# Seven rotating float32 pieces instead of three for the first unit's FFN activations, with the written-out order of all work replaced

## The chip, the cores and the metric

The kernel runs on one core of a Trainium2 chip. The metric is the device time of one execution in microseconds (us). The core has a matrix engine (TensorE, PE in the profile; PEld is its weight load), three elementwise engines (VectorE = DVE, ScalarE = ACT, GpSimd = POOL) and a queue engine (SyncE = SP) that issues transfers. Each works through its own instructions in order and waits on the others by semaphores. Matrix results go to PSUM banks, everything else lives in SBUF.

## The reference, cut to what matters

Attention whose mask comes from hash bits (batch 4, 8 heads, 768 tokens, head size 64), then a feed-forward network (FFN, 512 to 2048 to 512) on the 3072 tokens:

```python
q_bits = (np.einsum('bhsd,dk->bhsk', q, proj) > 0)
k_bits = (np.einsum('bhsd,dk->bhsk', k, proj) > 0)
mask = q_bucket[:, :, :, None] == k_bucket[:, :, None, :]
scores = np.where(mask, scale * q @ k.T, -1000000000.0)
attn = exp(scores - max) / (sum + 1e-09)
x = (attn @ v)                      # to [3072, 512]
h = x @ w_in
g = h * np.tanh(log1p(exp(h)))      # "mish"
return g @ w_out
```

## The kernel before

**Units.** The tokens are worked in 12 units of 256 (four batches of three). A unit has eight attention steps S, numbered 0 to 95 over the kernel, and eight FFN steps m, also 0 to 95. Most operands are split into a float16 high part and a float16 rest, and a product is three matmuls: high by high, high by low, low by high. In the first unit (FFN steps 0 to 7) the FFN instead runs in float32, with one matmul (L1120, L1169) where the later units have three (L1130 to L1132, L1179 to L1181).

**An attention step** S n: the scores of two heads for 128 queries on PE into the banks ps_s (L937, or L948 in float32), the row maximum on DVE (L978, "max"), a few tiny scale instructions ("mb", L961 to L973), two exponentials on ACT (L991), row sums and their reciprocal (L1015, L1021), then from unit 1 on the high part ("hi", L390 on POOL, L392 on ACT or L393 on DVE) and the rest ("lo", L408 on DVE or L414 and L415 on POOL), which transfers turn (DMA_TRANSPOSE), and for every fourth step the product with the values (V, L1088). From S 8 on there is one set of ps_s banks, so S n+1 can start only when both exponentials of S n have read them.

**An FFN step** m: H (24 matmuls, PE) into one of two accumulators acc0, acc1 in turn; mish on ACT out of it (L1151, in the first unit L1147) into a piece of the buffer ffb; from unit 1 on g_hi and g_lo, the float16 halves, into one of four other pieces; and two output products O m 0 and O m 1 (six matmuls each) into ps_o. After every eighth step the output is copied out ("ob", L1197 on ACT or L1203 on DVE) and stored.

**The buffer ffb** has nine pieces of 512 float32. Step m puts its mish into piece m % 3 (line `t = m % 3`). Pieces 3 to 6 hold the float16 halves of the steps of unit 1 and later (3 + m % 4), which the first unit does not have. Piece 7 begins with a unit matrix.

**Tables.** exp and mish lie in different tables of ScalarE. A change is an ACT_TABLE_LOAD (L1315), which `Plan.ordered` puts in wherever the next exp or mish in the order is not of the table that is loaded.

**The order.** Nothing is scheduled at build time. Every operation is registered with its predecessors, worked out from the regions that it reads and writes, and gets a number. ORDER is a written-out list of all 2636 numbers. A letter after a number picks an engine among the operation's alternatives (none is the first, b the second and so on). Each engine's program is its part of this list. The numbers used below: S 15, 16, 17 are 493, 533, 553, and the maximum of S 16 is 534; S 20 and 21 are 659 and 691; S 24, 25, 26, 27 are 794, 826, 842, 871; mish of m 0 to 7 are 398, 400, 457, 459, 524, 526, 587, 589; the four part copies of the last output are 2634, 2632, 2629, 2627. Two tiny matmul groups use a shared bank: a statistic "st" (621) and the hash bits "hp" (568, 627).

```python
if o.kind and o.kind != table:
    table = o.kind
    load(table)
```

Of the kernel before, what the change touches and what calls it, by code (L numbers as in the profile page):

```python
# [93 lines left out]
137 7 9 8 50 20 0 5 11 19 12 22 1 2 3 4 76 80 29 81b 13 37 6 77b 14 15 10 25 33 26 30b 38 17 27 28 18 34 39 52  # L94
60 61 35 62 41 56 54 63 57 55 21 42 48 51 53 24 23 31 78 36 32 64 65 16 86 91 138 92 79 87 147 40 88 82 117 83
43 118 44 119b 93 89 66 109 110 111 153 90 94 120 67 112 154b 132 107d 46 108 133 113 95 115 68 114 116 124
125b 155 121 126 101 84 45 134 136 135 156 127b 178 96 128 140b 148 141 47 58 149 85 122d 123 97 99 142 139b
98b 143 129 168d 179 180d 100 174 176 69 175 177 170 130 157 171b 131 172 173b 204 205b 169 70 145b 182 189
144b 102 158 159 181 161b 190b 71 193 291 194 195 185 191 150 186 192 220 221 103 222d 183b 187 206 160b 196
188 197 104 223 212 152 146 49 151 162 59 105 106 213b 207 216 218 217b 219b 214 215b 184 353 224 243 163 239  # L100
164 244 245b 241 248 240 242 233c 270 368 307 210d 208 235 254 236 255 249 209b 237 246 238 247 225 256 271
250 257 234 272d 262 263 268 266 292 198 273 226 267b 211 227 293 165 294 269 251 283 284 349 350 264 303 265
285 295 166 304b 354 305 296 258 199 200 309d 286b 310 311c 260c 261 306 274 281 313 253 252 232 228 282 312b
322 201 317 364 287 365 288 289 290 366 318 319 355b 323 324 308 320 321 367 330b 331 315 338 339 72 231 203
202 167 229 397 369b 314 329 316 325 297 298b 275 276b 340 333 341 230 332b 334 342 73 370d 299 336 425c 277
74 426 371 399 378 379 380 335 328 302 400 398 300 373 424 423 351 337 301 280 381 427 372b 374 382 389c 411
376 259 375 278 279 406 429 458 428 390 412 452 407 352 391 383 384b 393 392c 395 326 327 385 453 408d 409 410
415d 343 344c 356c 416 451 430 456 345 431 432 394 377 459 386 418 346 457 396 401 417b 454 433 387 348 347
413 419 455 75 357 434 443d 488b 460 421 444 461 420 388 422 441 404 435 436 414 402 445 489 490b 447 437 462d
# [5 lines left out]
589 597 613 599 580 363 618 600 560 561 562 614d 616 584b 615 632c 563 564c 601 566 651 508 509 585 633 647  # L115
634c 648 655 659 640 617 567 649 636 650 652 664 653 605 635 656 565 619 620 621 660 654 638 622 623c 625 568
569 602 639 661d 609 668 606 641 663 662 681b 682 683c 642 626 637 570b 691 607b 608 685 657 665 666 571b 627
692 628 693d 572 624b 643b 782 672 644 645c 646 695 694 669 610b 658 723c 724 629 630b 684b 687 696 734 735
670b 673 783 697 675 725b 727 736d 738 686 726 631 698 737 688 690 689 732 786 731 749 674 667 699c 701 729
740d 741 791 742c 744 676 728 787 788 700 750 751 702 730 745 799 703 704 706 743b 677b 671 678 746 739 733  # L120
# [1225 lines left out]
```

## Time and profile before

| what | us |
|---|---|
| median of 3 runs (lowest, highest) | 817.67 (816.54, 818.07) |
| the profiled execution, own time | 817.2 |
| its span in the profile | 815.4 |
| PE busy in the span | 798.2 |
| ACT busy | 624.9 |
| DVE busy | 602.9 |
| POOL busy | 426.9 |

The profiled execution's time is 1.8 us above its span; all sums over the trace are made against the span. A matmul's busy time contains its way through the array, so neighbouring matmuls overlap: a busy PE says that no gap was seen, and not that it ran at its peak. Idle time is put down to the engine and line whose semaphore came last.

### The profile page before, as it was taken

The numbers are of one execution on the slowest core, as the hardware profiler recorded it, in microseconds if no ns is written. First come the engines' busy times: TensorE is split into PE (matmuls) and PEld (weight loads), VectorE is DVE, ScalarE is ACT, GpSimd is POOL, SyncE is SP. The second block draws the span as 40 slices with busy tenths as digits, with TensorE's granted clock in tenths as the row PEclk, the third lists the DMA queues.
The fourth block names the chain that finished last, engine by engine and source line by source line (L and its number), as shares of the span: only waits on it lengthen the run. The fifth ranks groups of instructions, "written<-read, shape, count | busy, mean of one in ns | idle before, by whom it ended". The sixth has DMA issues, their size and how long they took to land.

```text
span 815.4 us, 17000 instructions
## 1 busy us (share of the span) xinstructions
PE 798.2 (98%) x6546; PEld 549.6 (67%) x6546; DVE 602.9 (74%) x1103; ACT 624.9 (77%) x976; POOL 426.9 (52%) x434
## 2 busy tenths in 40 slices
PE   8899999999999999999999999999999999999998
PEld 5556666666676776676666676667676676776674
DVE  5888999988898778887887767768877675566211
ACT  4889998888696769889679698989779785677211
POOL 3564446554356773733585564344646758845120
PEclk9999999999999999999999999999999999999999
DMA  7958998989999969989989959999989577466200
GB/s 253 219 174 221 240 246 196 191 156 206 217 160 182 203 116 181 170 158 216 185 172 155 195 117 151 197 213 192 167 140 169 107 139 145 81 124 133 50 27 27
DMA packets 395489, 134.29 MB, mean 165 GB/s; under 512 B 365456, under 2 KB 386448, under 8 KB 395408
## 3 DMA queue, kind: packets, MB, share of 16 engines
q1 hardware_dynamic: 395408, 133.21, 81.2%
q8 instruction: 51, 0.84, 0.4%
q14 instruction: 30, 0.25, 0.1%
HBM read 35.65 MB, written 6.29 MB: 51 GB/s over the span
## 4 chain that ended last, share of the span: by engine, by line
PE 47%; ACT 1%; DVE 1%; DMA 1%; issue 0%; POOL 0%; SPq 0%; ACTq 0%; DVEq 0%
PE ps_s L937 7%; PE ps_o L1179 6%; PE ps_o L1181 6%; PE ps_o L1180 6%; PE ps_acc L1130 5%; PE ps_t L1088 5%; PE ps_acc L1132 5%; PE ps_acc L1131 5%; ACT pb L991 1%; DVE svb L978 1%; DMA out_dram<-ffb 1%; PE ps_t L739 0%; ACT L1315 0%; DVE hl L408 0%; ACT tok L480 0%
## 5 line engine op out<-in xcount | busy, mean ns | idle before, releaser
L991 ACT ACTIVATE pb<-ps_s,svb 128x768 f32<-128x768 f32 x184 | 180.9, 987 | 87.4 <-DVE svb L968 36.7
L978 DVE TENSOR_REDUCE svb<-ps_s 128x2 f32<-128x1536 f32 x92 | 161.3, 1753 | 40.2 <-PE ps_s L937 33.7
L1130 PE MATMUL ps_acc<-X,wo 128*128 128x256 f16 x616 | 167.9, 273 | 0.3 <-ACT ffb L1151 0.3
L1132 PE MATMUL ps_acc<-X,wo 128*128 128x256 f16 x616 | 167.9, 273 | 0.0
L1131 PE MATMUL ps_acc<-X,wo 128*128 128x256 f16 x616 | 167.9, 273 | 0.0
L1315 ACT ACT_TABLE_LOAD x117 | 150.1, 1283 | 2.0
L408 DVE SCALAR_TENSOR_TENSOR hl<-pb,svb,hl 128x768 f16<-128x768 f32 x131 | 140.3, 1078 | 13.8 <-POOL hl L390 9.8
L1181 PE MATMUL ps_o<-wi,ffb 128*128 128x512 f16 x352 | 133.4, 379 | 0.0
L1180 PE MATMUL ps_o<-wi,ffb 128*128 128x512 f16 x352 | 133.4, 379 | 0.0
L1179 PE MATMUL ps_o<-wi,ffb 128*128 128x512 f16 x352 | 133.4, 379 | 0.0
L937 PE MATMUL ps_s<-KT,QT 128*128 128x512 f16 (+1 forms) x656 | 120.1, 326 | 2.1 <-ACT pb L991 1.8
L390 POOL TENSOR_SCALAR hl<-pb,svb 128x768 f16<-128x768 f32 x68 | 71.0, 1046 | 75.9 <-DVE svb L1021 28.8
L937 PEld LDWEIGHTS <-QT 128*128 128x128 f16 x672 | 64.2, 98 | 40.5 <-issue 8.3
L1088 PE MATMUL ps_t<-PT,VT 128*64 128x256 f16 x1584 | 90.7, 273 | 0.0
L1088 PEld LDWEIGHTS <-VT 128*64 128x64 f16 x1584 | 84.8, 110 | 8.1 <-issue 7.6
L1151 ACT ACTIVATE ffb<-ps_acc,smalls 128x512 f32<-128x512 f32 x88 | 58.5, 684 | 33.5 <-PE ps_acc L1132 32.0
L415 POOL TENSOR_TENSOR hl<-pb,hl 128x768 f16<-128x768 f32 x45 | 75.0, 1667 | 3.8
L414 POOL TENSOR_SCALAR pb<-pb,svb 128x768 f32<-128x768 f32 x45 | 44.4, 987 | 48.0 <-ACT hl L392 21.4
L1131 PEld LDWEIGHTS <-wo 128*128 128x128 f16 x616 | 60.2, 98 | 13.3 <-issue 1.5
L1130 PEld LDWEIGHTS <-wo 128*128 128x128 f16 x616 | 60.2, 98 | 12.6 <-issue 0.5
L1132 PEld LDWEIGHTS <-wo 128*128 128x128 f16 x616 | 60.2, 98 | 7.0
L1181 PEld LDWEIGHTS <-ffb 128*128 128x128 f16 x352 | 34.4, 98 | 41.6
(240 smaller groups left out, 1300.5 us busy)
## 6 DMA issues: line engine op xcount, KB each, us to landing
out_dram<-ffb SPq DMA_DIRECT2D x22, 256.0 KB, 2.7
stg<-in_v_dram SPq DMA_DIRECT2D x13, 384.0 KB, 4.0
stg<-in_k_dram SPq DMA_DIRECT2D x12, 384.0 KB, 4.0
wo<-in_q_dram SPq DMA_DIRECT2D x9, 512.0 KB, 4.9
stg<-in_moe_w_in_dram SPq DMA_DIRECT2D x8, 512.0 KB, 4.6
stg<-in_moe_w_out_dram SPq DMA_DIRECT2D x6, 512.0 KB, 4.6
PT<-hl SPq DMA_TRANSPOSE x176, 4.1
wo<-in_moe_w_out_dram SPq DMA_DIRECT2D x5, 512.0 KB, 4.7
```

The lines of the kernel that those rows point to most:

```text
L408: return [("DVE", 215 + 1.035 * n, port(lambda: nc.vector.scalar_tensor_tensor(out=dst, in0=src, scalar=sc, in1=hi, op0=ALU.mult, op1=ALU. ...
L937: nc.tensor.matmul(ps[:, hh * S + c0 * P:hh * S + c1 * P], QTb[:, u % 2, sl, qi], KTb[:, j, sl, hh * NCH + c0:hh * NCH + c1].rearrange("p ...
L978: op("max", [("DVE", 1755, lambda: nc.vector.tensor_reduce(out=sv[:, 0], in_=ps.rearrange("p (h e) -> p h e", e=S), axis=AX.X, op=ALU.max, ...
L991: EXP[n, hh] = op("exp", [("ACT", 1075, lambda hh=hh, t=t: nc.scalar.activation(pb[:, t], HOMES[n][0][:, hh * S:(hh + 1) * S], AF.Exp, bia ...
L1088: nc.tensor.matmul(pv[hh * D:(hh + 1) * D, y * 256:(y + 1) * 256], vt[:, w, hh * NCH + c], pt[:, hh, a * NCH + c].rearrange("p s t -> p (s ...
L1130: nc.tensor.matmul(o, wh, X[:, 0, c], start=(c == 0), stop=False)
L1131: nc.tensor.matmul(o, wh, X[:, 1, c], start=False, stop=False)
L1132: nc.tensor.matmul(o, wl, X[:, 0, c], start=False, stop=(c == NCC - 1))
L1179: nc.tensor.matmul(PS[f"o{s}"], gh, wh, start=first, stop=False)
L1180: nc.tensor.matmul(PS[f"o{s}"], gh, wl, start=False, stop=False)
L1181: nc.tensor.matmul(PS[f"o{s}"], gl, wh, start=False, stop=last)
L1315: for fn in plan.ordered("exp", lambda x: nc.scalar.preload_act_table_set(sets[x])):
```

## The change

In the first unit, step m now uses piece m % 7 instead of m % 3, so pieces 3 to 6, which only later units used, take part. Later units keep m % 3. The ORDER list is another one throughout: the same 2636 numbers, in other places and in part with other engine letters. No operation is added or removed apart from the table loads that follow from the order. The code, and the parts of the list around the steps named above ("..." marks what is left out):

```diff
-463 464 478d 403 446c 449 479 405 465 438 466b 471 472b 487 523 518 493 494 495c 486 358 359 467 496 480b 482b
-497 448 481b 484 360 491 510 525 532 511 442 450 361 512b 533 534 535 362 526 524 468 483 513b 492 439 546 514
-474 536 552 485 469 470 537 519b 475c 476 516 473 520 538c 539 553 515 517 586 540b 521 554 440 477 498 499b
...
-500 501 555d 542 522 541c 556 557 573b 574 575 548 549b 550 527 503 502 544 577 590 545 543 578 528 530 504
-505b 591 592 547 588 506 594 593 507 576b 595d 587 581 612 603 604 551 582 583b 579 596 598c 529 559 558 531
...
-634c 648 655 659 640 617 567 649 636 650 652 664 653 605 635 656 565 619 620 621 660 654 638 622 623c 625 568
-569 602 639 661d 609 668 606 641 663 662 681b 682 683c 642 626 637 570b 691 607b 608 685 657 665 666 571b 627
...
-803 781 752 753 773b 800 784c 774 776 775 785 790 679b 804 705b 707 708 710 709 711 794 748 824 712 801c 779
-777b 795 796c 802b 789 713 792 714c 716 780 747 778 825 839 680 798 797 816c 817 818b 715b 819 826 827 828 829
-820 822 830 807 808 842 611 717 754 755 821 847 823 810 831b 832 833b 809 811 756 757 805 843 844 845 835 846
-840 718 859 841 836 834c 719 721b 720b 758 759 860 722 760 837 838 769 861 871 872 863 873b 874 812 862b 864
...
-2608 2603 2607b 2602 2621 2609 2613 2614c 2610b 2611 2616 2617 2618b 2619b 2615 2623 2620 2625 2622 2576 2631
-2579 2634b 2635 2632b 2633 2624 2626 2629b 2627 2630 2628
...
+447 464 487 523 493 446 402 489 437 438 465 466b 403 449b 478 494 479 480c 482 405 495d 496 497 448 481b 450
+442 518 525 439 533 467 526 524 468 483 356c 472c 440 510d 473 511 484 534 535 512b 490 470 469 514 474 536
+475 537 515 485 486 492 359 546 553 513 491 538d 360 539 476 516 519b 520 521 477 498 499b 554 541 540b 500
...
+517 501 542 522 548c 544 555d 557 556 573c 574 362b 575c 577 549 550 552 586 527 587 528 590 547 503 502 504
+505b 529 591 592 543 506 576c 551 578 545 588 581 530 594 593 507 531 508 582b 579 612 559 558 604 603 589 560
...
+561 361 509 583 648 595d 596 597b 598b 613 599 647 614d 615 616 562 363 580 600 618 651 659 609 640 655 563
+564c 566 601 649 652 567 617 632d 633 634 636b 584c 650 585 635 565 605b 660 638 619 620 606 641 656 607b 661d
+621 622 623 653c 654 625 664 568 668 663 662 681c 637 639 602 626 569 608 643c 644 682 645c 691 692 690 627
...
+704 790 705b 706 745 752 707 678 785 709 753 746 710 773c 774 775c 794 777 789 795 800 776b 711 779b 747 778
+780 847 801 781 825 712 748 840 796 798 797 802 713 714c 791 716 816c 804 715c 680 817 819b 805 826 827 828
+818c 820 806 829 830 831c 807 824 717 754 822 808 832 833c 835b 642 755 810 756 757 821 834b 823 836 809 842
+843 811 839 859 718 769 844 837 812c 719 841 884 758 845 846 759 760b 871 887 770 868 891 860d 721b 720b 861
...
+2609 2605 2606b 2610c 2607 2612 2611b 2613 2621 2616 2614 2615 2623 2620 2625 2622 2576 2579 2617 2618 2619
+2631 2634b 2635 2632b 2633 2624 2626 2629b 2627b 2630 2628
...
@@ ffn_mish
-        t = m % 3
+        t = m % (3 if u else 7)
         tr = ("ff", t * 512, (t + 1) * 512)
@@ ffn_out
-        w = (3 + m % 4) * 512 if u else (m % 3) * 512
-        g32, w32 = ffb[:, m % 3], at(HOME[1, g])
+        w = (3 + m % 4) * 512 if u else (m % 7) * 512
+        g32, w32 = ffb[:, m % 7], at(HOME[1, g])
```

Counted over the two lists:

| | before | after |
|---|---|---|
| table changes in all | 117 | 113 |
| of these ahead of S 32 | 24 | 26 |
| groups of mish in the first unit | 1,0 / 3,2 / 5,4 / 6,7 | 0,1 / 3,2 / 5,4 / 6 / 7 |
| g_hi on ACT, POOL, DVE | 34, 34, 20 | 30, 30, 28 |
| hi on ACT, POOL, DVE | 53, 68, 55 | 54, 60, 62 |
| scale instructions "mb" on DVE, POOL | 74, 22 | 64, 32 |

More of the change, by code (lines that the diff above doesn't have):

```diff
@@ L99 @@
[L99 to L103, printed above, removed]
@@ new lines @@
+910 906b 869 912 940 968 941 930b 932 969 942 943 854 903 931c 934 855 976 851b 945d 946 856 1027 907b 857b
+921 972 954 933 948b 955 970c 947 956d 949 958 1028 957 886 935 858 937 936 982 944 951 950 959c 977 938 973
+986 967 960 961b 962b 963 978 1066 979 980 981 995c 974c 983 964 952 965 971 1029c 966 1031b 1005 1004 996 987
+1006 1030c 997c 999 1007d 1008 1009 975b 998 1001b 990 991 992 1010b 1011 1012b 993 994 1021 953 1022 1192
+1193 1032 1194 984b 1014 1023b 1024 1025 1000 1002 1015 1019 1033 1069 1003 1050 1013c 1016b 1034 1039b 1040
@@ new lines @@
+985 1051 1041b 1017 870 1223 1195 988b 1070 1018 1038 1196 1082 1073 1042b 1052d 1053 1043 1054 1055c 1044
+1056 989 1057c 1059 1045b 1058c 1046 1060 1077 1061b 1078 1079c 1083 1074 1081 1080 1063 1020 1086 1064 1035b
+1067 1068 1071c 1072 1075c 1197 1036 1084c 1095c 1096 1098b 1097 1099b 1062 1105 1047 1090 1106 1107c 1108
+1109 1101 1110 1085 1111 1121 1122 1087 1091 1048 1076b 1198 1112c 1123 1124 1114 1125 1150 1151 1088b 1127d
+1037 1065 1100 1113c 1158 1116 1102 1154 1136 1104 1103 1128 1092 1200 1155 1137 1115 1117 1129b 1130c 1138
@@ new lines @@
+1131 1139 1132 1140 1141c 1133 1093 1142 1143b 1145 1134 1146 1119 1168 1159 1160 1161 1163 1162 1177c 1144b
+1147 1152c 1153 1126 1118 1164 1178 1094 1169 1179 1187 1188 1189 1190 1181 1191 1207c 1208 1148 1049 1201
+1120 1172 1180b 1183b 1156 1089b 1165 1166 1157b 1209c 1211 1218 1199 1219 1220b 1173 1175 1224 1182 1210b
+1213b 1184 1252 1212 1174 1225 1176 1226c 1222 1221 1236d 1237 1238 1149 1135 1240b 1228 1186 1185 1216 1202
+1247 1282 1215 1278 1248 1249c 1250 1251 1203 1239c 1205 1214 1253 1229 1241 1286 1204b 1242 1267d 1170 1171
@@ new lines @@
+1409 1361 1388 1263 1389 1390c 1264b 1265b 1392b 1410 1411b 1406 1399c 1414 1347 1327 1346 1412 1413 1431c
+1462 1360 1391c 1394 1362 1393 1395 1266 1441 1348 1354 1403c 1298 1328 1329c 1432 1331 1442 1443c 1433b 1435
+1444 1369 1363 1422 1332 1307 1400b 1445 1446c 1434c 1437 1370 1415 1423 1447 1425 1419 1416c 1448b 1330b
+1450b 1424 1426 1371 1372 1396 1457 1333 1334 1458 1440 1439 1459b 1373 1502 1374 1335b 1404 1336b 1460 1461
+1375 1475 1476 1377 1438 1436 1449 1451 1486 1337 1378 1506 1477 1503 1504b 1515 1379 1454 1452 1407 1479 1487
@@ new lines @@
+1563 1584 1536 1535 1473 1550 1552 1551 1572 1562b 1564 1573 1574c 1597 1559 1428 1527 1566 1429b 1575 1430
+1565 1501 1576 1592 1553 1601 1582 1577 1585c 1578b 1643 1644 1593 1594 1567 1596 1595 1610c 1580 1586 1646
+1681 1611 1579 1568 1620 1618 1621 1645 1598 1613 1599b 1622b 1616 1581 1485 1605 1619 1683 1589 1600 1590
+1623 1647 1612b 1614b 1624 1625 1626 1627c 1629b 1615 1636 1628b 1631b 1633 1634 1635 1606 1637 1607 1638c
+1868 1630 1617 1632 1608 1602 1609 1648 1603 1653 1640 1639 1654c 1655 1656 1657c 1665 1666 1667 1668 1658
@@ new lines @@
+1904 1886 1905 1923c 1888 1846 1850 1859 1890 1871 1933 1887 1889 1924 1847b 1925b 1872 2020 1848b 1894 1873
+1898 1926c 1927b 1934 1860 1935b 1906 1895b 1936 1937 1914 1964 1929 1875 1919c 1953d 1954 1896 1955b 1891
+1965 1917 1915 1916 1966 1957 1920 1899b 1907 1967 1968 1970c 1900b 1849 1938 1930 1928 1876 1910 1932 2012
+1979 1931 1958 1939 2077 1971 1972c 1956 1959 1918 2021 1974 1874b 2013 1940 1911 1973 1941 1980 1877 1878
+2014c 1921 1981d 1879b 1961 1962 1942 1982 1983 1976 1922 1943 1880 1908 1909 1944c 2016 2029 2003d 2017 1912c
@@ new lines @@
+1975 1960 1985 1881 2004 1946 2005c 2007 2024 2025 2026c 2028 2027 2046c 1984 1947 1977 2033 1969 1963 2008
+1948 2056 1949 2015 2018 2006b 1945b 1913b 2011 1986 1987 1951 2057 2009b 2010 1950b 2019b 1988 1978 2055 1989
+2047 2048c 2034 2030 2031b 2049 1990c 2058 2050 2060 2059 2061c 1992 2052 1999 2032 2062 2063c 2037 2072 1861
+1952 1991b 2038 2040 2039 2041 1993 2051 2053 2070 1994 2121 2089 2073 2022 2074 2078 2065b 2075 2076 2064b
+2122 2090d 2035 2036b 1995 2067 2079 2080 2091 2092 2066 2101 1892 2068 2102 2103 2093 2104 2094 2105 2106c
@@ new lines @@
+2117 2000 2114 2054 2082 2107 2096 2023 2125 2069 2134 2071 2126 2001 2206 2002 1996b 2127d 2108 2128 2110
+2129 2123 2143d 2095 2097 2083 2118 2109c 2111 2153 2098 2144 2112 2296 2044c 1997 2084 2085 2154 2155c 2145
+2146c 2147 2156 2115b 2042c 2157 2113 2256 1998 2130 2138 2119 2149 2120 2081c 2158b 2159 2160c 2169 2099 2131
+2045b 2141 2132b 2135 2086b 2133b 2162 2170 2171b 2257 2139 2172 2173 2136c 2150 2148 2161c 2043 2087 2175
+2124 2164 2176 2163 2151 2198 2202 2184 2203 2185 2177b 2178 2199 2179 2297 2186 2188 2181 2137 2088 2165 2166
@@ new lines @@
+2484 2548 2519 2520c 2510c 2499 2551 2515 2509b 2511b 2482 2485c 2513 2514 2512 2522 2521 2524c 2549c 2525
+2486 2550b 2533 2516 2555 2523 2517 2546 2488 2552 2527b 2530b 2490 2526 2528 2553c 2534 2535 2537 2536 2538b
+2539 2529 2541b 2544 2540 2554b 2532 2569 2568 2556 2557b 2558b 2542 2531 2465 2489 2491 2559 2570 2560 2571
+2545 2543 2561c 2562 2572 2573 2563 2577 2574 2564 2565 2566 2567 2580 2581 2582 2584 2585 2586c 2583b 2588
+2592 2589 2578b 2575b 2590c 2593 2594b 2587b 2591b 2595b 2597 2596 2599 2608 2601 2598 2603 2600 2604 2602
```

155 lines of the change are left out of this document (57 added, 98 removed).

## The prediction

> **What bounds the kernel now.** I read the page's busy line first, then busy time by stage (the cuts are the starts of S 0, 10, 20, 31, 64 and 95), then PE in order of time.
>
> ```profile
> span 815.4 us, 17000 instructions
> PE 798.2 (98%) x6546; PEld 549.6 (67%) x6546; DVE 602.9 (74%) x1103; ACT 624.9 (77%) x976; POOL 426.9 (52%) x434
> ```
>
> ```profile
> 0.00:14.90 14.90, 11.84 (x111) 9.02 (x112) 6.71 (x24) 6.78 (x13) 4.62 (x11) 1.00 0.76 265
> 14.90:71.60 56.70, 51.28 (x426) 32.86 (x424) 47.34 (x94) 46.91 (x96) 30.45 (x36) 1.00 0.78 206
> 71.60:158.40 86.80, 86.09 (x523) 58.64 (x522) 80.64 (x121) 79.35 (x119) 44.08 (x39) 1.00 0.98 217
> 158.40:249.50 91.10, 88.13 (x799) 62.50 (x797) 81.88 (x151) 75.02 (x116) 42.42 (x47) 1.00 0.99 188
> 249.50:502.00 252.50, 251.26 (x2150) 174.54 (x2148) 197.30 (x361) 206.57 (x317) 148.07 (x144) 1.00 0.89 169
> 502.00:744.80 242.80, 242.80 (x2068) 168.25 (x2067) 171.38 (x324) 191.15 (x289) 143.46 (x143) 1.00 0.81 152
> 744.80:815.40 70.60, 66.80 (x483) 43.80 (x481) 17.68 (x31) 19.16 (x30) 13.76 (x15) 1.00 0.20 44
> ```
>
> The columns are length, then busy time of PE, PEld, DVE, ACT and POOL, then clock and transfers. Length less PE busy is what PE stood idle: 3.06, 5.42, 0.71, 2.97, 1.24, 0 and 3.80 us, 17.2 in all. So PE sets the time from S 10 on, and whatever is taken off another engine can win at most these gaps. A busy PE could still be a slow one; the order of time shows its pace:
>
> ```profile
> 183.62 0.27 PE L1130 MATMUL ps_acc<-X,wo 128*128 128x256 f16 x1
> ...
> 186.24 0.38 PE L1179 MATMUL ps_o<-wi,ffb 128*128 128x512 f16 x1
> ...
> 187.53 1.46 PE L937 MATMUL ps_s<-KT,QT 128*128 128x512 f16 x8
> 188.84 0.27 PE L1130 MATMUL ps_acc<-X,wo 128*128 128x256 f16 x1
> ```
>
> From start to start, H takes 2.62 us, an O 1.29, an S 1.31, one behind the other without a hole. The change keeps all of this PE work. What it can move is where PE waits:
>
> ```profile
> 171.35 0.46 PE L739 MATMUL ps_t<-pj,KT 128*128 128x12 f16 x12 [0.72 <-DVE hl L408]
> ```
>
> ```profile
> 206.11 0.59 PE L937 MATMUL ps_s<-KT,QT 128*128 128x512 f16 x2 [0.57 <-ACT pb L991]
> ```
>
> ```profile
> 212.03 0.38 PE L937 MATMUL ps_s<-KT,QT 128*128 128x512 f16 x1 [0.41 <-ACT pb L991]
> ```
>
> ```profile
> 217.95 0.59 PE L937 MATMUL ps_s<-KT,QT 128*128 128x512 f16 x2 [0.24 <-ACT pb L991]
> ```
>
> ```profile
> 241.22 0.38 PE L937 MATMUL ps_s<-KT,QT 128*128 128x512 f16 x1 [0.45 <-ACT pb L991]
> ```
>
> These five (before the hash of entry 627, S 25, S 26, S 27, S 30) are 2.39 of the 2.97 us idle between S 20 and S 31.
>
> **The change part by part.** *The seven pieces.* They free the first unit's mish of the wait for the O that last read its piece. There is no such wait to remove: the eight float32 mish waited 0.7 us in all, for their own H.
>
> ```profile
> L1147 ACT ACTIVATE ffb<-ps_acc 128x512 f32<-128x512 f32 x8 | 4.4, 595 | 0.7 <-PE ps_acc L1120 0.7
> L1315 ACT ACT_TABLE_LOAD x117 | 150.1, 1283 | 2.0
> L991 ACT ACTIVATE pb<-ps_s,svb 128x768 f32<-128x768 f32 x184 | 180.9, 987 | 87.4 <-DVE svb L968 36.7 <-DVE svb L965 24.2 <-POOL svb L973 11.7
> L978 DVE TENSOR_REDUCE svb<-ps_s 128x2 f32<-128x1536 f32 x92 | 161.3, 1753 | 40.2 <-PE ps_s L937 33.7 <-PE ps_s L948 3.5 <-ACT tok L480 1.8
> L408 DVE SCALAR_TENSOR_TENSOR hl<-pb,svb,hl 128x768 f16<-128x768 f32 x131 | 140.3, 1078 | 13.8 <-POOL hl L390 9.8 <-ACT hl L392 3.0
> L392 ACT ACTIVATE hl<-pb,svb 128x768 f16<-128x768 f32 x53 | 48.7, 929 | 14.3 <-DMA PT<-hl 6.7 <-DVE svb L978 2.6 <-ACT pb L991 2.6
> L393 DVE TENSOR_SCALAR hl<-pb,svb 128x768 f16<-128x768 f32 x55 | 39.9, 726 | 4.0 <-DMA PT<-hl 3.2
> L607 DVE SCALAR_TENSOR_TENSOR wi<-wi 128x1024 int32<-128x1024 int32 x2 | 2.4, 1204 | 0.0
> ```
>
> Nor do they gather more: with two accumulators a third mish needs an H after the first, and the new list has five groups in the first unit where the old had four. So the change doesn't do what its ring is for, and that is part of my forecast, not a rival. Value 0.
>
> *Table changes.* 117 become 113, at 1.283 us each: 5.1 us less on ACT. Ahead of S 32 there are two more (+2.6), behind it six fewer (-7.7). Behind S 31 PE has only 1.24 us of idle time to give, spread over 495 us, so I take 0 for the six; if ACT did bound that stage they would be worth 7.7. The two more fall where ACT has 7.45 and 16.08 us idle (the third and fourth stage): 0, at most +2.6.
>
> The Trainium skill ("ScalarE: Activation LUTs", What ACT_TABLE_LOAD costs) gives a change about 2.66 us: 1283 ns and a drain of 1380 ns. By it the two early ones would cost 5.3 us on ACT and speak against the change; the trace below has the first ACTIVATE 1.30 us after the load's start (195.52 less 194.22), so no such drain is seen here.
>
> *The waits at S 25, S 26, S 27.* ACT between the exponentials of S 23 and S 24:
>
> ```profile
> 194.22 1.28 ACT L1315 ACT_TABLE_LOAD   x1
> 195.52 0.69 ACT L1151 ACTIVATE ffb<-ps_acc,smalls 128x512 f32<-128x512 f32 x1
> 196.10 1.76 ACT L392 ACTIVATE hl<-pb,svb 128x768 f16<-128x768 f32 x2
> 197.77 0.92 ACT L392 ACTIVATE VT<-stg,smalls 128x768 f16<-128x768 f32 x1
> 198.60 0.66 ACT L1151 ACTIVATE ffb<-ps_acc,smalls 128x512 f32<-128x512 f32 x1
> 200.20 0.84 ACT L480 ACTIVATE tok<-stg 128x768 bf16<-128x768 f32 x1 [0.94 <-DMA stg<-in_k_dram]
> ...
> 201.76 0.84 ACT L480 ACTIVATE tok<-stg 128x768 bf16<-128x768 f32 x1 [0.62 <-DMA stg<-in_v_dram]
> ...
> 202.71 1.28 ACT L1315 ACT_TABLE_LOAD   x1
> 204.01 0.99 ACT L991 ACTIVATE pb<-ps_s,svb 128x768 f32<-128x768 f32 x1
> ```
>
> The new list takes out of this chain two "hi" (1.76), one v_hi (0.92) and one mish (0.66): 3.3 us, against a wait of 0.57. The gap before it holds about 1.0 us more of ACT work in the new list, so the wait is gone even if the two loads come as late as now; 1.7 us later (3.3 - 1.0 - 0.57) it would be back. After it, S 25 to S 26 and S 26 to S 27 each took 5.92 us by the rows above (206.11, 212.03, 217.95), which is how long scores, maximum and exponentials need. PE had S and V, then S, three O and two tiny groups, in between. The new list adds one O to each (entries 824 and 884), 1.29 us against waits of 0.41 and 0.24: both gone. The hash of entry 627, now directly behind S 21, gets an O (690) in front: 1.29 against 0.72, gone. Together -1.94, bounds -1.94 and 0.
>
> *What is late next.* S 28 to S 30: the old list has 16.1 us of PE work (9.49 and 6.65, from the paces above) and 16.6 of ACT work there, and 0.45 of wait. The new one has 13.5 and 14.4, an excess of 0.9: +0.45 (0 to 0.9). S 16: its maximum (534) follows its S at once in the old list; in the new one seven DVE jobs come first, two w_join (1.20 each), one lo (1.08) and four short ones. Much of it runs while PE still works on S 16: +0.3 (0 to the 3.5 us of the three). S 92 to S 93: PE work falls from 9.1 to 6.5 us while ACT gets two mish, two high parts and two table loads, 7.9 us with its exponentials; the work before it leaves some slack: +0.2 (0 to 1.4).
>
> *Engine letters.* 24 tensor_scalar jobs move to DVE (hi 7, g_hi 8, w_hi 4, v_hi 3, q_hi and k_hi 1 each), and ten "mb" leave it. DVE is idle in front of a maximum for 40.2/92 = 0.44 us on the mean; a "hi" takes 0.73. So one that lands ahead of a maximum makes it 0.29 late. I take +0.5 (0 to 2.5, worked out under the rivals).
>
> *The first 71.6 us.* 8.48 us of idle time, mostly turns through one bank. Pairs of turns with at most 0.33 us of other PE work between them: eight in the old list, six in the new, but more of these directly behind each other. Value 0, a quarter of the 5.42 either way (1.4).
>
> *The end.*
>
> ```profile
> 809.05 0.88 DVE L1203 TENSOR_SCALAR ffb<-ps_o,smalls 128x256 f32<-128x256 f32 x2 [9.60 <-PE ps_o L1181]
> 811.64 0.48 DVE L1203 TENSOR_SCALAR ffb<-ps_o,smalls 128x256 f32<-128x256 f32 x1 [1.71 <-PE ps_o L1181]
> ```
>
> ```profile
> 812.16 0.47 ACT L1197 ACTIVATE ffb<-ps_o,smalls 128x256 f32<-128x256 f32 x1 [8.08 <-DVE ffb L1203]
> ```
>
> The last copy moves from ACT to DVE: two on DVE took 0.88, the mixed pair 0.99 (812.63 less 811.64): -0.1.
>
> *Sum.* -1.94 - 0.1 + 0.45 + 0.3 + 0.2 + 0.5 = -0.6, on the profiled execution's 817.2: 816.6, which stands 1.1 us under the runs' median of 817.67.
>
> **The rivals.** *Faster:* nothing takes the place of the waits removed, and the first 71.6 us give their 1.4: 817.2 - 2.04 - 1.4 = 813.8; with the early part alone at 0, 815.2. For it: 27 gaps between scores have under 6.7 us of PE work in the new list (S 20 on; 21 in the old), but none is under 5.92, where the old had two. Against: the early DVE work grows.
>
> *Slower:* the jobs moved to DVE put off row maxima. Place: the gaps between scores of under 6.7 us, 27 of 75. Price: 24 x 27/75 x 0.29 = 2.5 us, which with the gains lost is 819.7. It decides from the point where DVE's idle time in front of L978 falls under what a moved job adds, 0.29 a step. For it: DVE is busy 81.88 of 91.10 and 80.64 of 86.80 us in the two stages between S 10 and S 31. Against: behind S 31 it is busy 78% and 71%.
>
> *ScalarE sets the time behind S 31:* six loads fewer give -7.7, 809.5. Against it: PE's missing gaps there. The Trainium skill ("Perfetto Trace Analysis", Identifying the Most-Contended Engine) would leave room for it: it calls matmul busy share a bad measure and takes weight-load busy, which is 67% here. The pace of 1.29 an O without holes speaks for a full PE all the same.
>
> **How the numbers follow.** 0.2% (1.6 us) is about what a measurement of this kernel can tell from no change, so 816.0 to 819.3 is the same. My forecast, 816.6, lies in it: 0.40. Faster: 0.33 for the first rival, 0.03 for ScalarE. Slower: 0.24 for DVE. The range runs from 812.6 (the first rival's 813.8, and the 1.24 us behind S 31 returned as well) to 820.6 (the slower case and the 0.9 that S 28 to S 30 can cost). The forecast's own range is 815.2 (the waits removed, nothing added) to 818.6 (the waits come back elsewhere and the four added terms, 1.45, stay).
>
> **What would show it.** Right: no wait on L991 of over 0.2 us at S 25, S 26 and S 27; 113 table loads; ACT's busy time down by some 5 to 10 us with PE's unchanged at 798; idle PE behind S 31 still under 2.5 us. Wrong: a wait in front of S 17 or S 30 of over a microsecond; waits of PE on DVE behind maxima all over; or a first stage whose S 10 starts over 1.5 us away from 71.6.

## The result, and the profile after

The changed kernel takes 824.62 us (median of 5 runs, 823.31 to 826.62), the kernel before in the same session 817.08 (816.54 to 818.07): a ratio of 1.0094, interval 1.0077 to 1.0110, so 7.7 us slower (7.5 by the medians). The profiled execution took 825.72, with a span of 823.9, 8.5 over the span before.

The page after, its span and TensorE's busy line:

```profile
span 823.9 us, 16988 instructions
PE 800.2 (97%) x6546; PEld 550.0 (67%) x6546; DVE 613.2 (74%) x1082; ACT 614.4 (75%) x967; POOL 390.8 (47%) x424
```

ScalarE lost 10.5 us of work and GpSimd 36; VectorE got 10.3 more. TensorE, which sets the time, is busy 2.0 us longer with the same 6546 matmuls, and idle 23.7 us in place of 17.2. Busy time by stage, cut at the starts of S 0, 10, 20, 31, 64 and 95 as in the prediction (length, then busy time of PE, PEld, DVE, ACT and POOL, then clock and transfers):

```profile
0.00:14.80 14.80, 11.12 (x106) 8.13 (x106) 4.64 (x21) 5.54 (x13) 2.58 (x8) 1.00 0.85 274
14.80:73.70 58.90, 52.18 (x430) 33.38 (x428) 48.75 (x95) 49.14 (x99) 29.43 (x43) 1.00 0.76 203
73.70:158.40 84.70, 83.35 (x498) 56.50 (x497) 79.83 (x120) 79.13 (x117) 34.63 (x38) 1.00 0.94 211
158.40:250.50 92.10, 90.58 (x822) 64.50 (x821) 82.59 (x140) 77.33 (x120) 47.37 (x48) 1.00 1.00 192
250.50:508.00 257.50, 252.53 (x2149) 175.23 (x2148) 196.44 (x355) 196.84 (x306) 137.26 (x145) 0.99 0.90 167
508.00:750.80 242.80, 241.05 (x2058) 167.31 (x2057) 183.10 (x326) 187.62 (x289) 116.66 (x121) 1.00 0.79 149
750.80:823.90 73.10, 69.36 (x495) 44.97 (x493) 17.88 (x31) 18.83 (x27) 22.91 (x23) 1.00 0.25 51
```

Length less PE busy: 3.68, 6.72, 1.35, 1.52, 4.97, 1.75 and 3.74 us idle, where before had 3.06, 5.42, 0.71, 2.97, 1.24, 0 and 3.80. One stage got better, S 20 to S 31, by 1.45 us. Two stages that had almost no idle time now have it: S 31 to S 64 gained 3.7 us of it, and S 64 to S 95 1.75. PE in order of time, the larger of its waits from S 4 on and the one at S 25 (in brackets how long, and for what):

```profile
37.77 1.24 PE L937 MATMUL ps_s<-KT,QT 128*128 128x512 f16 x7 [0.83 <-DMA KT<-wo]
...
121.34 0.81 PE L948 MATMUL ps_s<-KT,QT 64*128 64x256 f32 x6 [0.76 <-ACT pb L991]
...
206.62 1.46 PE L937 MATMUL ps_s<-KT,QT 128*128 128x512 f16 x8 [0.25 <-ACT pb L991]
...
272.54 1.46 PE L937 MATMUL ps_s<-KT,QT 128*128 128x512 f16 x8 [0.87 <-ACT pb L991]
...
469.71 2.72 PE L937 MATMUL ps_s<-KT,QT 128*128 128x512 f16 x8 [2.54 <-ACT pb L991]
...
500.10 1.46 PE L937 MATMUL ps_s<-KT,QT 128*128 128x512 f16 x8 [0.75 <-ACT pb L991]
...
552.95 1.46 PE L937 MATMUL ps_s<-KT,QT 128*128 128x512 f16 x8 [0.74 <-ACT pb L991]
...
567.20 0.16 PE L496 MATMUL ps_t<-smalls,ones 128*128 128x2 bf16 x1 [0.55 <-ACT tok L480]
```

The first stands inside S 4, the others in front of S 16, S 25, S 34, S 59, S 63, S 70 and of the hash of the token squares before S 72. The largest by far is S 59: it waits 2.54 us for exponentials, and then takes 2.51 us from start to start of the next group (472.22 less 469.71) in place of 1.31. What ScalarE and VectorE did ahead of it:

```profile
458.96 0.47 ACT L1096 ACTIVATE X<-ps_t,smalls 128x256 f16<-128x256 f32 x1 [0.26 <-PE ps_t L1088]
463.81 0.47 ACT L1096 ACTIVATE X<-ps_t,smalls 128x256 f16<-128x256 f32 x1 [4.38 <-DVE X L1099]
464.30 1.28 ACT L1315 ACT_TABLE_LOAD   x1
465.60 0.69 ACT L1151 ACTIVATE ffb<-ps_acc,smalls 128x512 f32<-128x512 f32 x1
466.30 1.28 ACT L1315 ACT_TABLE_LOAD   x1
467.60 0.99 ACT L991 ACTIVATE pb<-ps_s,svb 128x768 f32<-128x768 f32 x1
```

```profile
461.63 1.76 DVE L978 TENSOR_REDUCE svb<-ps_s 128x2 f32<-128x1536 f32 x1 [1.87 <-PE ps_s L937]
463.30 0.47 DVE L1099 SCALAR_TENSOR_TENSOR X<-ps_t,smalls,X 128x256 f16<-128x256 f32 x1
```

Here X is the normalized output of one attention group, in a high part (x_hi, ACT, L1096) and a low part (x_lo, DVE, L1099), two of each from one bank of TensorE's results. The second x_hi reads nothing that x_lo writes, and yet ACT stood 4.38 us in front of it until the first x_lo was done. That x_lo stands in the list behind the row maximum of S 58, which itself waited 1.87 us for S 58. With ACT stood a mish, two table changes and the exponentials of S 58, and behind those S 59. In the kernel before, ACT waits for an x_lo in front of an x_hi for 0.3 us in all.

### The profile page after: what moved, and what is told of

Read it like the earlier page. It is cut to its first block, busy times and chain, and to the rows that moved or that the text cites. A ratio compares the mean times of both kernels' runs of the same rounds, so it can differ in the third digit from the quotient of the medians.

```text
span 823.9 us, 16988 instructions
## 1 busy us (share of the span) xinstructions
PE 800.2 (97%) x6546; PEld 550.0 (67%) x6546; DVE 613.2 (74%) x1082; ACT 614.4 (75%) x967; POOL 390.8 (47%) x424
## 4 chain that ended last, share of the span: by engine, by line
PE 41%; ACT 3%; DVE 3%; issue 2%; DMA 2%; POOL 1%; SPq 0%; DVEq 0%; ACTq 0%; POOLq 0%
PE ps_s L937 6%; PE ps_o L1179 5%; PE ps_o L1181 5%; PE ps_o L1180 5%; PE ps_acc L1130 5%; PE ps_acc L1131 5%; PE ps_acc L1132 5%; PE ps_t L1088 4%; ACT pb L991 1%; DVE svb L978 1%; DMA PT<-hl 1%; ACT L1315 1%; DMA KT<-tok 1%; ACT ffb L1151 0%; DVE hl L408 0%
## 5 line engine op out<-in xcount | busy, mean ns | idle before, releaser
L991 ACT ACTIVATE pb<-ps_s,svb 128x768 f32<-128x768 f32 x184 | 180.9, 987 | 99.2 <-DVE svb L968 50.5
L408 DVE SCALAR_TENSOR_TENSOR hl<-pb,svb,hl 128x768 f16<-128x768 f32 x132 | 138.1, 1053 | 15.0 <-POOL hl L390 6.1
L390 POOL TENSOR_SCALAR hl<-pb,svb 128x768 f16<-128x768 f32 x60 | 65.3, 1090 | 106.4 <-DVE svb L1021 62.9
L415 POOL TENSOR_TENSOR hl<-pb,hl 128x768 f16<-128x768 f32 x44 | 73.7, 1675 | 3.7
L414 POOL TENSOR_SCALAR pb<-pb,svb 128x768 f32<-128x768 f32 x44 | 41.7, 947 | 62.8 <-ACT hl L392 35.0
```

The costliest lines, as they stand in the source:

```text
L408: return [("DVE", 215 + 1.035 * n, port(lambda: nc.vector.scalar_tensor_tensor(out=dst, in0=src, scalar=sc, in1=hi, op0=ALU.mult, op1=ALU. ...
L991: EXP[n, hh] = op("exp", [("ACT", 1075, lambda hh=hh, t=t: nc.scalar.activation(pb[:, t], HOMES[n][0][:, hh * S:(hh + 1) * S], AF.Exp, bia ...
```

## The experiments

Spans are those of the profiled executions; ratios are to the kernel before, with their 95% intervals.

| run | time, us | ratio | interval | span |
|---|---|---|---|---|
| the changed kernel | 824.62 | 1.0094 | 1.0077 to 1.0110 | 823.9 |
| e1_ring: rotation over seven, old order but for entry 609 | 823.20 | 1.0069 | 1.0052 to 1.0085 | 820.8 |
| e5_ring1: old order word for word, m7 in piece 1 | 816.29 | 0.9993 | 0.9984 to 1.0002 | 814.4 |
| e2_s58: changed, one x_lo moved | 820.80 | 1.0040 | 1.0026 to 1.0054 | 818.5 |
| e6_hi: changed, one x_hi moved | 820.45 | 1.0046 | 1.0032 to 1.0059 | 818.2 |
| e3_first: old, new order to S 10 | 820.17 | 1.0039 | 1.0026 to 1.0052 | 817.3 |
| e4_mid: old, new order S 10 to S 57 | 817.66 | 1.0004 | 0.9994 to 1.0013 | 816.0 |
| e8_part: old, new order S 18 to S 31 | 816.19 | 0.9988 | 0.9979 to 0.9997 | 814.1 |
| e7_fix: changed, four places mended | 822.02 | 1.0065 | 1.0050 to 1.0081 | 819.8 |
| e9_mend3: changed, three places mended | 820.09 | 1.0035 | 1.0024 to 1.0047 | 819.1 |
| e11_letter: e2, one engine letter back | 819.14 | 1.0028 | 1.0018 to 1.0038 | 817.7 |
| e10_oldfirst: e9, old order to S 18 | 818.10 | 1.0015 | 1.0005 to 1.0024 | 817.7 |
| e12_best: old, new order S 18 to S 57 | 815.79 | 0.9987 | 0.9979 to 0.9996 | 813.9 |

### The rotation by itself

The theory was that the loss lies in the order; the rival, that it lies in the seven pieces. The old list does not quite fit them: mish m9 of the second unit takes piece 9 % 3 = 0, and m7 of the first now takes 7 % 7 = 0 (before, 7 % 3 = 1), so m9 has to wait for both O of m7. Entry 609, one of these, had to go ahead of entry 656, the mish m9.

```diff
-        t = m % 3
+        t = m % (3 if u else 7)
...
-... 605 635 656 565 619 620 621 660 ... 661d 609 668 ...
+... 605 635 609 656 565 619 620 621 660 ... 661d 668 ...
```

> The seven pieces with the order of before (one output product, entry 609, is put ahead of the mish of m 9, entry 656, because with seven pieces m 9 would else overwrite the piece of m 7 before that product has read it). If the loss sits in the order: 817 us within 1.6 us of before, ratio 0.998 to 1.002. If the ring itself costs (a new wait in front of the mish of m 9, or the pieces' place): 819 us or more.

Measured: 823.2, a ratio of 1.0069, all of it at one place: the span is 5.4 us longer than before's, of which PE waits 3.4 us more and is busy 2.0 us longer, behind the wait shown here (the last section says why). ACT of e1_ring, and PE:

```profile
166.10 0.69 ACT L1151 ACTIVATE ffb<-ps_acc,smalls 128x512 f32<-128x512 f32 x1 [5.46 <-PE ps_o L1169]
```

```profile
169.49 0.16 PE L496 MATMUL ps_t<-smalls,ones 128*128 128x2 bf16 x1 [3.43 <-ACT tok L480]
```

Mish m9 waits 5.46 us for the O (L1169) that reads piece 0; behind it in ACT's queue stand a copy and the squares, and PE stands 3.43 us in front of the hash of these squares. So the rotation carries a cost of its own in the old order, and the seven pieces have to be told apart from where m7 is put:

```diff
-        t = m % 3
+        t = m % 3 if u or m == 7 else m
...
-        w = (3 + m % 4) * 512 if u else (m % 3) * 512
-        g32, w32 = ffb[:, m % 3], at(HOME[1, g])
+        w = (3 + m % 4) * 512 if u else (1 if m == 7 else m) * 512
+        g32, w32 = ffb[:, 1 if m == 7 else m % 7], at(HOME[1, g])
```

> The rotation alone, with the old order word for word: the first unit's m0 to m6 in pieces 0 to 6, and only m7 in piece 1 (as with three pieces) in place of piece 0. Theory (the ring's price is that m7 sits in piece 0, which m9 of the next unit wants; without that the four more pieces neither win nor cost anything): the time of before, 817.1, within 0.2%, and no wait in front of the squares' matmul before S 21. Rival 1 (the pieces themselves win, because mish waited for its piece in the old order): 815 to 816. Rival 2 (the other constraints of the ring, the second unit's high and low parts in pieces 3 to 6, cost as well): 819 to 823, with the wait of 3.4 us before S 21 as in the run with entry 609 moved.

Measured: 816.29, 0.9993 (0.9984 to 1.0002), no difference that can be told. In ACT of e5_ring1 the mish of before's place and time is back, with no wait:

```profile
160.09 0.68 ACT L1151 ACTIVATE ffb<-ps_acc,smalls 128x512 f32<-128x512 f32 x1
```

The four more pieces win or cost nothing that these runs can tell (the interval leaves room for a gain of 1.3 us and a loss of 0.2); the 5.46 us of e1_ring is one shared piece. This settles the rotation in the old order only. The new list keeps to the constraint (both O of m7 stand ahead of m9), and what that cost its order was not measured by itself.

### S 58 and S 59

```diff
-... 1606 1637 1607 1638c ...
+... 1606 1607 1637 1638c ...
```

1606 is the first x_hi, 1637 the maximum of S 58, 1607 the first x_lo, 1608 (a few entries on) the second x_hi.

> The changed kernel with one entry moved: the first x_lo of unit 6's third value product (1607) stands ahead of the row maximum of S 58 (1637) instead of behind it. If the loss at S 59 to S 63 comes from the second x_hi waiting on ScalarE for this x_lo: the wait of PE in front of S 59 (2.54 us) and the slow clock behind it go, 819.5 to 821 us, some 4 to 5 us less than the changed kernel. If the stage is slow because VectorE has more work there: no change, 824 to 825 us.

Measured: 1.0040 in place of 1.0094, 4.4 us less (0.0054 of 817). This does not yet say why x_lo was wanted early: for itself, or for the x_hi behind it. The next run leaves DVE's order alone and moves the x_hi.

```diff
-... 1606 1637 1607 1638c 1868 1630 1617 1632 1608 ...
+... 1606 1637 1608 1607 1638c 1868 1630 1617 1632 ...
```

> The changed kernel with one entry moved: the second x_hi (1608, ACT) ahead of the first x_lo (1607, DVE). DVE's order is untouched, the row maximum (1637) stays ahead of x_lo. Theory (the second x_hi waits for x_lo only because x_lo stands ahead of it in the list and reads the same bank; x_hi itself needs nothing from DVE): no wait of 4.4 us at that x_hi, S 59 on time, 820 to 821.5, as in the run that moved 1607. Rival (what is late is x_lo itself, so the row maximum must not stand ahead of it): 824 to 825, no change.

Measured: 1.0046, 3.9 us less, the same gain within the intervals. ACT and DVE of e6_hi:

```profile
457.41 0.83 ACT L1096 ACTIVATE X<-ps_t,smalls 128x256 f16<-128x256 f32 x2
```

```profile
459.94 1.76 DVE L978 TENSOR_REDUCE svb<-ps_s 128x2 f32<-128x1536 f32 x1 [1.37 <-PE ps_s L937]
461.62 0.48 DVE L1099 SCALAR_TENSOR_TENSOR X<-ps_t,smalls,X 128x256 f16<-128x256 f32 x1
```

Both x_hi now run in one go, and the x_lo still comes behind the maximum: its lateness never mattered. The rows show where the wait came from. In the changed kernel the first x_hi waits for PE (458.96) and the second, with the first x_lo ahead of it in the list, for DVE (463.81); in e6_hi, with no reader on DVE ahead of it, the second follows the first without a wait.

Between two engines that read the same tile of TensorE's results the program holds the order of the list with a wait. The Trainium skill ("PSUM — Partial Sum Buffer", PSUM bank collisions raise a hardware error) states that rule: instructions of different engines on one bank are kept apart by a dependency, reads against reads included. These rows agree with it. The kernel's own list of predecessors has no such edge, so nothing in the order's text shows it.

That the shared bank is the tie, and not the buffer X into which both write different parts, was not run by itself. The traces speak for the bank: hl is one buffer too, and in the kernel before, ACT's high part (L392) and DVE's low part (L408) of it run side by side 17 times, one of them at 196.95 and 197.07. And the prediction's own rows of the end show such a wait in the kernel before: two part copies read one bank and write different parts of ffb, and ACT's (812.16) began only when DVE's (811.64, 0.48 us) was done.

### Which parts of the order cost, and which win

Three splices of the two lists; entries that the first list has already issued are left out of the second.

```diff
-ORDER = before
+ORDER = after up to S 10, then before
```

> The kernel before with the new list up to S 10 and the old list for the rest (three pieces). If each stretch keeps its own gain or loss: +2.1 us, 819 us. If a loss that early is taken up later, where PE waits anyway: 817 us, no change.

Measured: 1.0039 (1.0026 to 1.0052), 3.2 us; the splice itself brought two new waits behind S 10 (1.10 and 0.84 us), so this bounds the first part from above.

```diff
-ORDER = before
+ORDER = before up to S 10, then after up to S 57, then before
```

> Old list up to S 10, new list from there up to S 57, old list for the rest, seven pieces. If each stretch keeps its own gain: the new list gained 1.0 us there, so 816 us, ratio 0.997 to 1.000. If VectorE's larger share of work costs everywhere: 819 us or more.

Measured: 1.0004, no difference, with 113 table changes. Here too waits stand right behind the first seam, 1.4 us up to S 12. At S 18 the two lists have issued almost the same entries, so the next splice is made there, with m7 in piece 1, so that both orders fit:

```diff
-ORDER = before
+ORDER = before up to S 18, then after up to S 31, then before
```

> The old order to S 18, the new one from S 18 to S 31, the old one behind; the rotation with m7 in piece 1, so that both orders can be used. 121 table loads where before has 117. Theory (the prediction's main terms: the waits before the hash of 627 and at S 25 to S 27 and S 30 go, 2.4 us, and 0.4 to 1 comes back at other places there): span 814 to 815.5 by PE's waits, 815.6 to 816.6 in time, 0.1 to 0.2% under before. Rival (the four more table loads and the seams take it back): 817 to 819.

Measured: 0.9988 (0.9979 to 0.9997), with 121 table changes. PE's busy time between S 18 and S 31, first of the kernel before, then of e8_part:

```profile
138.00:249.50 111.50, 108.36 (x914) 1.00 0.97 187
```

```profile
138.40:248.30 109.90, 108.53 (x913) 1.00 0.98 190
```

3.14 us idle against 1.37, 1.8 us less, and four more table changes did not take it back. How much of this is the order's is less sure. Between S 18 and S 31 e5_ring1, with the old order and the same pieces, idles 2.85 us, and e4_mid and e10_oldfirst, with the new order, 2.37 and 2.46. In time e8_part (816.19) can't be told from e5_ring1 (816.29), which was measured in the same session. One execution strays too: in e8_part's profile PE waits 1.54 us in front of S 15, where the list is still the old one and the kernel before waits 0.17.

### S 63, S 69 and S 71

```diff
-... 1606 1637 1607 1638c ...
+... 1606 1607 1637 1638c ...
...
-... 1706 1707 1699c 1737 1808 1715 1765 1708 ...
+... 1706 1708 1707 1699c 1737 1808 1715 1765 ...
...
-... 1926c 1927b 1934 1860 1935b ...
+... 1934 1935b 1926c 1927b 1860 ...
...
-... 2013 1940 1911 1973 1941 ...
+... 1940 2013 1941 1911 1973 ...
```

> The changed kernel with four places mended in the list: 1607 ahead of 1637 (S 58's maximum), 1708 (second x_hi) ahead of 1707, S 69's maximum and its mb (1934, 1935) ahead of hi 1926 on DVE, and the squares 1940 and 1941 ahead of two mish. Theory (each place costs by itself what PE waits there): 3.8 + 0.5 + 0.8 + 0.7 less than the changed kernel's 824.6, so 818.8, with the waits at S 59, S 63, S 70 and in front of the squares' matmul before S 72 under 0.4 us each. Rival (the slack is gone behind S 57, and a wait mended there comes back at the next S): 820.5 to 821, as with the first of the four alone.

Measured: 1.0065, worse than with the first mend alone (1.0040). The waits at S 70 and before S 72 were gone, but S 63, where the second x_hi had been freed in the same way as at S 59, waited 2.40 us in place of 0.75. PE, VectorE and GpSimd of e7_fix at that place:

```profile
495.46 2.08 PE L937 MATMUL ps_s<-KT,QT 128*128 128x512 f16 x8 [2.40 <-ACT pb L991]
```

```profile
488.77 1.91 DVE L393 TENSOR_SCALAR ffb<-ffb,smalls 128x512 f16<-128x512 f32 x1
```

```profile
488.75 1.64 POOL L415 TENSOR_TENSOR hl<-pb,hl 128x768 f16<-128x768 f32 x1
```

and VectorE of e2_s58, where x_hi still waited and GpSimd's difference began behind this one, at 489.70:

```profile
489.36 0.54 DVE L393 TENSOR_SCALAR ffb<-ffb,smalls 128x512 f16<-128x512 f32 x1
```

The mend worked for ACT, and brought the g_hi on DVE forward into GpSimd's difference of two tensors (L415), beside which it took 1.91 us in place of 0.54. The maximum of S 62 stands behind it. So the next run keeps the other three mends and leaves 1708 where it was (the edit against e7_fix):

```diff
-... 1706 1708 1707 1699c 1737 1808 1715 1765 ...
+... 1706 1707 1699c 1737 1808 1715 1765 1708 ...
```

> The changed kernel with three places mended: 1607 ahead of 1637, S 69's maximum and mb (1934, 1935) ahead of hi 1926, the squares 1940 and 1941 ahead of two mish; 1708 stays where it was. Theory (in the run with four mends, S 63 alone got worse, because a g_hi on DVE there fell together with a tensor_tensor of GpSimd and took 1.91 us in place of 0.54; the other mends are worth what PE waited): 820.6 - 1.5 = 819.1, and 2 to 2.5 under the run with four. Rival (the mends at S 69 and S 71 are worth nothing, the time comes back behind them): 820.5.

Measured: 1.0035 (1.0024 to 1.0047). Under e7_fix by 2.4 us, as expected; against e2_s58 (1.0040) no difference can be told, where 1.5 us was expected. The waits at S 70 and before S 72 are gone, but one of their size has come up inside S 78, for a transfer. PE of e9_mend3:

```profile
614.53 1.24 PE L937 MATMUL ps_s<-KT,QT 128*128 128x512 f16 x7 [0.91 <-DMA KT<-tok]
```

So the rival held here in good part. What held S 70 back was tried once more by itself. DVE, GpSimd and ACT of the changed kernel there:

```profile
546.87 1.77 DVE L393 TENSOR_SCALAR hl<-pb,svb 128x768 f16<-128x768 f32 x1 [2.13 <-DMA PT<-hl]
548.56 1.74 DVE L978 TENSOR_REDUCE svb<-ps_s 128x2 f32<-128x1536 f32 x1
```

```profile
546.59 1.64 POOL L415 TENSOR_TENSOR hl<-pb,hl 128x768 f16<-128x768 f32 x1
```

```profile
550.84 0.99 ACT L991 ACTIVATE pb<-ps_s,svb 128x768 f32<-128x768 f32 x1 [3.13 <-DVE svb L968]
```

The high part (entry 1926) was on ACT before. On DVE it stands ahead of S 69's maximum, waits 2.13 us for a transfer to read its buffer out, then takes 1.77 us beside GpSimd's difference in place of about 0.6, and ACT stands 3.13 us in front of the exponentials. One letter, beside the mend of S 58:

```diff
-... 1926c 1927b 1934 ...
+... 1926 1927b 1934 ...
```

> The changed kernel with 1607 ahead of 1637 and one engine letter set back: the high part 1926, which stands ahead of S 69's maximum, on ACT as in the old order in place of DVE. Theory (on DVE it holds the maximum back while it waits for a transfer, on ACT it holds back nothing that is due): the wait of 0.8 us at S 70 goes, 820.6 - 0.8 = 819.8. Rival (on ACT the same transfer holds back the exponentials that stand behind it there): 820.6, the wait at S 70 stays.

Measured: 1.0028 (1.0018 to 1.0038), by the ratios 1.0 us under e2_s58, though the intervals overlap. The wait at S 70 fell from 0.74 to 0.25 us, and the one before S 72 is gone; inside S 78 one of 0.72 for a transfer came up, as in e9_mend3. The theory's number was met; the difference in time is at the edge of what can be told.

### The account

```diff
-ORDER = after with three mends
+ORDER = before up to S 18, then after with three mends
```

> The same three mends, and the old order to S 18 with m7 in piece 1; 113 table loads. Theory (the whole loss is made up of the first stage, +2 to 2.6, S 58 to S 59, +3.8, S 69 to S 72, +1.5, and some 0.9 at S 63; the rest of the new order is as good as the old, 1 us better at S 21 to S 57): 816.5 to 817.5, no change from before. Rival (something spread over the whole new order costs as well): 818.5 or more.

Measured: 1.0015 (1.0005 to 1.0024), between theory and rival: 1.2 us over the kernel before. Read from run to run, the 7.7 us are 4.4 at S 58 (changed to e2_s58), 0.4 at S 69 and S 71 (to e9_mend3), 1.6 in the part before S 18 (to e10_oldfirst), and 1.2 that stay. By the medians, each against before in its own session, they are 3.8, 0.3, 2.0 and 1.4. Only the 4.4 stands well clear of the intervals; the 1.6 just does, the 0.4 does not. The 1.2 were not taken apart: the trace of e10_oldfirst shows waits of 0.87 us at S 34, 0.74 at S 63, 0.76 just ahead of S 27 and, for a transfer, 1.03 before the keys' hash behind S 21, where before waits 0.72.

The last run joins the good parts, and mends S 34, whose exponentials waited for scale values from GpSimd behind a low part of 3.2 us:

```diff
-ORDER = before
+ORDER = before up to S 18, then after up to S 57, then before
...
-... 1006 1030c 997c 999 1007d ...
+... 1006 1007 1030c 997c 999 ...
```

> The old order to S 18, the new one to S 57, the old one behind; m7 in piece 1; and S 33's mb (1007) on DVE ahead of q_cp (1030) in place of GpSimd, where it stood behind a low part of 3.2 us. Theory (the new order is better by some 1.5 us at S 18 to S 31 and by 1 us at S 36 to S 57, and the mend takes 0.9 us away at S 34): a span of 813 to 814, 814.8 to 815.8 in time, 0.2% under before. Rival (what the middle wins is lost at the seams): 816.5 to 817.5.

Measured: 0.9987 (0.9979 to 0.9996): faster than both kernels by a little, and not to be told from e8_part or from e5_ring1 (0.9993). From S 18 to S 31 PE idles 1.62 us:

```profile
137.70:247.90 110.20, 108.58 (x914) 1.00 0.98 190
```

The mend at S 34 missed. PE, DVE and POOL of e12_best:

```profile
270.64 1.46 PE L937 MATMUL ps_s<-KT,QT 128*128 128x512 f16 x8 [1.62 <-ACT pb L991]
```

```profile
266.91 1.51 DVE L393 TENSOR_SCALAR hl<-pb,svb 128x768 f16<-128x768 f32 x1
```

```profile
266.73 1.27 POOL L415 TENSOR_TENSOR ffb<-ffb 128x512 f16<-128x512 f32 x1
```

GpSimd, free of the scale values, begins its next difference earlier, and the high part on DVE again falls beside it, 1.51 us in place of about 0.6. The second exponential waits for the low part behind that, and S 34 waits 1.62 us, more than the 0.87 of the changed kernel.

## Why the prediction was wrong

It said 816.6, range 812.6 to 820.6; the time was 824.62.

*What bounds the kernel.* Right: PE sets the time. But the idle time of a stage was read as what the change can win, and its smallness behind S 31 (1.24 us) as a sign that little happens there. A small idle time bounds a gain, never a loss: that is where 5.5 us of new idle time came up, S 31 to S 95.

*The step that failed: the order behind S 31.* Beside the table changes and the engine letters, moved entries behind S 31 were costed at nothing; the wait at S 59 that one of them brought, with the slow clock behind it, cost 4.4 of the 7.7 us. "Gaps between scores of under 6.7 us" was the only thing looked for. S 59 has nothing to do with a short gap, nor with a moved letter: its cause is x_lo behind a maximum and x_hi behind x_lo, an edge that the list of predecessors lacks. The prediction followed those predecessors, though its rows 811.64 and 812.16 show a wait of this kind.

*The seven pieces, value 0.* Right in number: 0.9993 with m7 in piece 1. Also right that they gather no more mish and that there was no wait to remove. Missed: the numbering puts m7 and m9 into one piece, which cost the old order 0.69%.

*Table changes, 0.* Held. 113 were done, ACT's work fell by 10.5 us, and the time did not follow; e4_mid with 113 takes the time of before, and e8_part with 121 is not slower but 0.12% faster. The rival by which ScalarE sets the time behind S 31, 809.5, falls.

*The waits at S 25 to S 27, -1.94, with +0.45 at S 28 to S 30.* Right in sum: idle time between S 20 and S 31 fell by 1.45 us (predicted 1.49). That the two come so close is in part luck, as the terms do not fit one by one and the traces of one order differ there by about a microsecond. The gain in time stays unsure, as said at e8_part. In parts: the hash of 627, S 26 and S 30 have no wait left; S 25 kept 0.25 of 0.57; S 27's 0.24 gave way to 0.46 in front of a hash just ahead of it; the 0.45 at S 28 to S 30 did not appear; waits of 0.33 (ahead of S 24) and 0.21 (in it) came up, which no term had.

*S 16, +0.3.* Mis-sized: 0.76 in the changed kernel. *S 92 to S 93, +0.2:* no wait of this size was seen there.

*Engine letters, +0.5 (0 to 2.5), and the slower rival.* The mechanism was met at one place, S 70, 0.74 us of PE's wait, and e11_letter's 1.0 us is within the term. As a rival (819.7) it had the sign right and the place wrong: at S 70 it is one job that waits 2.13 us for a transfer and then takes 1.77, not 24 that each take 0.29. The other letters were not set back one by one. The 0.73 us for a "hi" was a mean: in the kernel before one on DVE takes about 0.6 us alone and 1.86 at 384.92, beside GpSimd's difference of 384.72, with a maximum behind it.

*The first 71.6 us, 0 (1.4 either way).* Failed: S 10 starts at 73.7, 2.1 late. Counting pairs of turns through one bank did not see S 4's wait for the transfer of KT (0.83), nor the rest; e9_mend3 to e10_oldfirst puts 1.6 us on the part before S 18.

*The end, -0.1.* Idle time behind S 95 went from 3.80 to 3.74: nothing that counts.

Of what would show it right, three signs failed: L991 still held S 25 for 0.25 us, PE was busy 800.2 in place of 798, and idle PE behind S 31 came to 6.7 us by S 95, where under 2.5 was asked. Of what would show it wrong, two came: S 10 over 1.5 us away from 71.6, and, at S 70 alone, PE waiting behind a maximum. The likeliest outcome and its range rested on adding up seen waits; the largest term was a wait that the list of predecessors did not contain and that showed in the trace of before only in small (0.3 us at an x_hi) and at the end, where it was read as the price of a copy.

## What to carry to other kernels

When the order of work is rewritten, read the waits of the built program, not only the data's dependences: two engines that read one bank of results are held in the order of the list, so put the readers of one bank together by engine (both x_hi, then both x_lo), and none behind a job that waits for something else. A stage with hardly any idle time has nothing to win and everything to lose from a new order. A mend that moves one job forward can push it beside another engine's long one: both mends that failed here did so on that.

## What the runs showed of the hardware that was not expected

*A short pause can halve TensorE's clock.* Windows of the changed kernel around S 59 (columns as above, the granted clock behind the busy times):

```profile
466.90:469.70 2.80, 0.27 (x2) 0.00 (x0) 0.00 (x0) 2.75 (x6) 0.17 (x1) 0.91 1.00 187
469.70:471.00 1.30, 1.29 (x5) 0.61 (x5) 0.79 (x2) 1.07 (x2) 0.00 (x0) 0.50 0.00 0
471.00:472.30 1.30, 1.30 (x6) 0.61 (x5) 0.00 (x0) 0.06 (x1) 0.00 (x0) 0.50 0.00 0
472.30:473.50 1.20, 1.20 (x12) 1.00 (x10) 1.04 (x1) 0.00 (x0) 0.00 (x0) 0.88 0.00 0
```

After 2.54 us without a matmul the next 2.6 us ran at a clock of 0.50, which made S 59 1.20 us longer: part of the 2.0 us by which PE is busier. It came again in e7_fix after 2.40 us:

```profile
495.40:497.30 1.90, 1.84 (x8) 0.94 (x8) 0.81 (x2) 1.87 (x3) 1.62 (x3) 0.70 0.95 181
497.30:498.50 1.20, 1.20 (x6) 0.51 (x5) 0.86 (x1) 1.20 (x3) 1.12 (x2) 0.50 1.06 197
```

and in e1_ring after 3.43 us, but not in e12_best after 1.62:

```profile
270.60:272.00 1.40, 1.36 (x9) 0.83 (x9) 0.19 (x1) 1.18 (x2) 0.49 (x1) 1.00 0.99 189
```

nor in e8_part after 1.54 (1.00 behind it too). These are all the pauses of over 1.5 us between matmuls in the traces of these runs.

The rows also give how long the half clock stood, if it is taken to be either 1.00 or 0.50. A clock of 0.91 over the 2.80 us ahead of S 59 is 0.5 us at 0.50, and 0.88 over the 1.20 us behind is 0.3: so from 469.2 to 472.6. In e7_fix 0.70 over 495.40:497.30 and 0.73 over 498.50:500.50 give 496.2 to 499.6, and in e1_ring 0.63 over 169.40:171.00 and 0.91 over 173.00:174.30 give 169.8 to 173.2. That is 3.4 us each time, begun 2.0, 3.1 and 3.8 us behind the end of the last matmul (467.17, 493.06, 166.06); in e7_fix and e1_ring the work behind the pause still started at the full clock. So the price beyond the wait itself is not a share of the wait. By an estimate from these three it is at most half of 3.4 us, 1.7, and less where part of the stretch falls into the pause.

The Trainium skill ("TensorE: Matmul & The Clock Gate", What's actually happening) puts the half rate behind an idle window of about 3.4 us; the half rate agrees, and here pauses of 2.40 us were enough.

*DVE's tensor_scalar beside GpSimd's tensor_tensor.* 1.91 us in place of 0.54 in e7_fix, 1.51 in place of about 0.6 in e12_best, and 1.77 at S 70 of the changed kernel. When the DVE instruction began, GpSimd's had 1.62, 1.09 and 1.36 us left (488.75 + 1.64 less 488.77, and so on), and DVE's took 1.4, 0.9 and 1.2 us longer: it gave up nearly all that GpSimd had left, some 0.2 us less. The Trainium skill ("SBUF — State Buffer", SBUF: two separate sides) has the two engines share one pair of ports, held for a whole instruction; all three rows agree with it.
